# A third transform stage in three products, and stages placed otherwise over the steps of a fused FFT filter and gated FFN

## The chip, the core and the metric

The kernel runs on one core of a Trainium2 chip. The metric is device time in microseconds (us) of one execution; the median of three runs is 1530.87 us (1530.43 to 1530.92). On the core, TensorE multiplies matrices (PE in the profile; PEld is its weight load), VectorE (DVE), ScalarE (ACT) and GpSimd (POOL) work on whole tiles, and SyncE (SP) issues the DMA transfers of the steady part. Each engine takes its own instructions strictly in order.

## The reference

The input `x` has 8 batches of 3136 rows and 256 columns. Each batch goes through a Fourier filter along the rows, then through a gated feed-forward network with a convolution of width 3:

```
X = np.fft.rfft(x, axis=1)
y = np.fft.irfft(X * (filt_r + 1j * filt_i), n=3136, axis=1)
h = np.maximum(y @ w_in, 0)                      # 256 -> 1024
conv[s] = sum(conv_w[k] * h[s + k - 1] for k in 0, 1, 2)
out = (h / (1 + np.exp(-conv))) @ w_out          # 1024 -> 256
```

Everything is float32 in and out.

## The kernel before, in words

**The transform.** 3136 is 112 x 28, so the Fourier transform and its inverse are done in four stages of matrix products, each in 14 pieces (`NP`, number `q`) of 112 or 120 rows by 512. Stage 1 multiplies the input by a table from HBM and stores the result in HBM (`store_first`). Stage 2 multiplies by the constant `s2_sb`, and its result in PSUM is multiplied by the filter (`filt`): three VectorE instructions (L300 to L302) and one GpSimd addition (L303) give the tile `z`. Stage 3 multiplies `z` by the constant `s3_sb` (`by_row`, L277 and, for the last piece, L280); ScalarE copies its result out of PSUM (`store_plain`, L268) and SP stores it in HBM. Stage 4 loads that back in another order, multiplies by a table (`fourth`, L311), VectorE copies the result (L733), and ScalarE and GpSimd write `y` as a rounded high part and a rest.

**Products of parts.** A float32 number may be split in a high part that is rounded to the type `fp32r` (`hi_act`, ScalarE, L156) and the rest, the difference of number and high part (`lo_pool`, GpSimd, L162, or `lo_dve`, VectorE, L159). `mm3` (L185 to L187) replaces one float32 product by three `fp32r` products: high by high, high by rest, rest by high. The FFN uses it throughout; so does stage 2 from the third batch on (`second_split`), whose parts stage 1 has stored in two tensors, `a_dram` and `r_dram`. Stages 1, 3 and 4, and stage 2 of the second batch, are plain float32 products.

**The FFN.** The rows of all batches are cut into 50 units of 510 (`UO`), each with 8 slices (`NF`) of the 1024 hidden columns. One slice of one unit is a *step*; there are 400, numbered m. In step m, TensorE does the transform pieces planned for this step, then the first product of slice m (`inner`, 6 matmuls), then the second product of slice m-6 (`project`, 12 matmuls). The other engines do, in step m, for slices of earlier steps:

- ScalarE: relu in PSUM of slice m-1 (L557), the middle tap of m-1 (`centre`, L562, it writes a tile `t` of 4 buffers), the sigmoid of m-2 (L569), the rounding of m-3 (`round_g`, L156).
- VectorE: the two outer taps of m-1 (L566) and between them the gate of m-2 (L572, the last reader of that slice's PSUM tile `ps_h`, of which there are 3).
- GpSimd: the rest of m-4 (`rest_g`, L162), the last reader of that slice's `t`.

Whatever the transform pieces of step m-1 left in PSUM is taken out by VectorE and ScalarE at the start of their step m, ahead of the FFN work there; the GpSimd addition L303 stands ahead of `rest_g` too. Every eighth step (m mod 8 = 6) a unit is done: VectorE copies two tiles of results (`evacuate`, L611) ahead of all else in that step, and SP has their output transfers (L616, L629) ahead of this step's loads.

**The plan.** The transform of batch t (t from 1 to 7; batch 0 is transformed ahead of the steps) runs during the 48 steps from w = 48(t-1) on, in which the FFN works on batch t-1. The lists `at1`, `at2`, `at4` and the counter `used` set the step of each piece: stage 2 at 9 steps for 5 pieces from w+2 on (t = 1: 3 for 2, from 7), stage 3 three steps after its stage 2, stage 4 in steps w+33 to w+44. The 14 pieces of stage 1 of the *next* batch go where the fewest other pieces are: in every window of t from 2 on that is w+0, 1, 4, 6, 8, 10, 13, 22, 27, 29 to 32 and 45. Loads are asked for ahead by `want_in` (at most 3 tiles `tin` for stages 1 and 4), `want_table` (3 pieces ahead, 4 buffers) and `want_filter` (1 ahead, 2 buffers). Where a batch ends within a unit, `join_tail` and `join_head` put the rows of both batches into a tile `yx`.

Of the kernel before, what the change touches and what calls it, by code (L numbers as in the profile page):

```python
# [9 lines left out]
F32 = mybir.dt.float32  # L10
F32R = mybir.dt.float32r
I32 = mybir.dt.int32
# [8 lines left out]
D = 256  # L21
FF = 1024
KT = D // 128
NF = FF // 128
UO = 510
# [107 lines left out]
def tile_fft_filter_gated_ffn(  # L133
# [21 lines left out]
    def hi_act(dst, src):  # L155
        nc.scalar.activation(dst, src, AF.Copy)  # L156
# [4 lines left out]
    def lo_pool(dst, src, hi):  # L161
        nc.gpsimd.tensor_tensor(out=dst, in0=src, in1=hi.bitcast(F32), op=ALU.subtract)  # L162
# [21 lines left out]
    def mm3(ps, wh, wl, rh, rl, start=True, stop=True, **kw):  # L184
        nc.tensor.matmul(ps, lhsT=wh, rhs=rh, start=start, stop=False, **kw)  # L185
        nc.tensor.matmul(ps, lhsT=wh, rhs=rl, start=False, stop=False, **kw)  # L186
        nc.tensor.matmul(ps, lhsT=wl, rhs=rh, start=False, stop=stop, **kw)  # L187
# [12 lines left out]
    wc = ctx.enter_context(tc.tile_pool(name="wc", bufs=1))  # L200
    s2_sb = wc.tile([112, 120], F32, name="s2_sb")
    s2s_sb = wc.tile([112, 120], F32, name="s2s_sb")
    second_parts = [[wc.tile([112, 120], F32R, name=f"{n}{h}") for h in range(2)] for n in ("s2", "s2s")]
    s3_sb = wc.tile([120, 112], F32, name="s3_sb")
    s3s_sb = wc.tile([120, 112], F32, name="s3s_sb")
    cw = wc.tile([128, 3, NF], F32, name="cw")
# [1 line left out]
    nc.scalar.activation(cw[:, 0, 0:1], cw[:, 0, 0:1], AF.Sigmoid)  # L208
    wi = [wc.tile([128, KT, FF], F32R, name=f"wi{h}") for h in range(2)]
    wo = [wc.tile([128, NF, D], F32R, name=f"wo{h}") for h in range(2)]  # L210
    turned = [wc.tile([120, 2, D], F32, name=f"v{k}") for k in range(2)]
    for v in turned:
        nc.gpsimd.memset(v[32:64], 0.0)

    tp = ctx.enter_context(tc.tile_pool(name="tp", bufs=2))
# [11 lines left out]
    NP = 14  # L227
# [47 lines left out]
    def by_row(o, q, r, m, ms):  # L275
        if q < NP - 1:
            nc.tensor.matmul(o, lhsT=m, rhs=r.rearrange("p j d -> p (j d)"), start=True, stop=True)  # L277
        else:
            for j, t in ((0, m), (1, ms)):
                nc.tensor.matmul(o[:, j * D:j * D + D], lhsT=t, rhs=r[:, j], start=True, stop=True)  # L280
# [9 lines left out]
            for j, parts in enumerate(second_parts):  # L290
                mm3(ps[0:120, j * D:j * D + D], *parts, r[:, 0, j], r[:, 1, j])

    def third(ps, q, z):
        by_row(ps[0:112], q, z, s3_sb, s3s_sb)

    def filt(ps, q, f, last=False):

# [18 lines left out]

    AHEAD = 6
    raws = {}
    conv_raw = tp.tile([128, 1, 6 * NF], I32, name="conv_raw", bufs=1)

    def load_weights(k, pool):
        if pool is tp:
# [39 lines left out]
    with (  # L362
# [16 lines left out]
        def bank():  # L379
            return sps.tile([128, 512], F32, name="ps")  # L380
# [22 lines left out]
        with tc.tile_pool(name="sq", bufs=2) as sq:  # L403
# [8 lines left out]
            def tab(kind, q):  # L412
                return tabs[kind, q // 2][:, 2 * (q % 2):2 * (q % 2) + 2]
# [22 lines left out]
            for q in range(NP):  # L436
# [6 lines left out]
                ps = turned_stage(rows["x", q // 2][:, 2 * (q % 2):2 * (q % 2) + 2], [tab("1", q)[:, j] for j in range(2)])  # L443
# [11 lines left out]
            for i in range(NP + 4):  # L455
# [34 lines left out]
        for q in range(NP + 1):  # L490
# [3 lines left out]
            if q:  # L494
                ps = bank()
# [10 lines left out]
    wp = ctx.enter_context(tc.tile_pool(name="wp", bufs=2, reuse_waits="tile"))  # L506
# [6 lines left out]
    NU = -(-LEN // UO)  # L513
    ts, hs, gs, pos, joined = {}, {}, {}, {}, {}
# [9 lines left out]
    def place(u):  # L524

        b, tok = divmod(UO * u, ROW)
        return b, tok, min(UO, LEN - UO * u)

    def joins(u):
        _, tok, n = place(u)  # L530
        return tok + n > S

    def join_tail(u):
        b, tok, n = place(u)
        joined[u] = [wp.tile([128, KT, UO + 2], F32R, name=f"yx{h}", bufs=1) for h in range(2)]
        for t, y in zip(joined[u], ys[b]):
            nc.gpsimd.tensor_copy(t[:, :, 0:ROW + 1 - tok], y[:, :, tok:ROW + 1])

# [93 lines left out]
    NW = 6 * NF  # L632
    plan, tails, heads = {}, {}, {}

    def put(m, kind, b, q):
        plan.setdefault(m, []).append((kind, b, q))

    for t in range(1, B):
        w = NW * (t - 1)
        used = [0] * NW  # L640
        if t == 1:
            at1 = [q // 2 for q in range(NP - AHEAD)]
            at2, at4 = [7 + 3 * q // 2 for q in range(NP)], [34 + 11 * q // NP for q in range(NP)]
            for q, s in enumerate(at1):
                put(s, "1", 1, AHEAD + q)
                used[s] += 1
        else:
            at2, at4 = [2 + 9 * q // 5 for q in range(NP)], [33 + 12 * q // NP for q in range(NP)]
        for q in range(NP):
            for s, kind, cost in ((at2[q], "2", 3), (at2[q] + 3, "3", 1), (at4[q], "4", 1)):  # L650
                put(w + s, kind, t, q)
                used[s] += cost
        if t + 1 < B:
            spots = []
            for q in range(NP):
                s = min(range(4 if t == 1 else 0, NW - 2), key=lambda s: (used[s], s))
                used[s] += 2
                spots.append(s)
            for q, s in enumerate(sorted(spots)):
                put(w + s, "1", t + 1, q)  # L660
        tails[w + 29] = heads[w + 46] = next(u for u in range(NU) if joins(u) and place(u)[0] == t - 1)
        assert NF * tails[w + 29] >= w + NW
    order = [(m, op) for m in sorted(plan) for op in plan[m]]
    inputs = [op for _, op in order if op[0] in "124"]
    tables = [op for _, op in order if op[0] in "14"]
# [1 line left out]
    got_in, got_table, got_filter, got_z, banks, vs = {}, {}, {}, {}, {}, {}  # L667
# [18 lines left out]
    def want_table(n):  # L686
        for op in tables[n:n + 1]:
            src = {"1": s1, "4": m2}[op[0]]
            got_table[op] = t = tp.tile([112, 2, 112], F32, name="tab", bufs=4)
            nc.sync.dma_start(out=t, in_=src[0:112, pair(op[2])])  # L690

    def want_filter(n):
# [4 lines left out]
    done, wanted = {"in": 0, "table": 0, "filter": 0}, {"in": 0}  # L697
    def transform(op):
        kind, b, q = op
        banks[op] = ps = ps_t.tile([128, 512], F32, name="ps_t")  # L700
        if kind in "124":
            done["in"] += 1
            r = got_in.pop(op)
        if kind in "14":
            want_table(done["table"] + 3)
            done["table"] += 1
            w = got_table.pop(op)
        if kind == "1":
            by_column(ps, w, r)
        if kind == "2":  # L710
            want_filter(done["filter"] + 1)
            done["filter"] += 1
            (second_split if b > 1 else second)(ps, q, r)
        if kind == "3":
            third(ps, q, got_z.pop((b, q)))
        if kind == "4":
            fourth(ps, r, w)

# [16 lines left out]
    def to_y(op):  # L735
        kind, b, q = op
        if kind == "4":
            v = vs.pop(op)
            yh, yl = y_slices(b, pair(q))
            hi_act(yh, as_y(v))  # L740
            return lambda: lo_pool(yl, as_y(v), yh)
        return lambda: None

    with tc.manual_schedule(engines=COMPUTE | {mybir.EngineType.SP}):
        want_in()
        for n in range(3):
            want_table(n)
        for m in range(NF * NU + PLAG + 1):
            p1, p2, p3, p4, p6, p7 = (at(m - k) for k in (1, 2, 3, 4, PLAG, PLAG + 1))
            new, old = plan.get(m, []), plan.get(m - 1, [])  # L750
            if p7:
                evacuate(*p7)
            if m == NF:
                for (h, l), t in zip(second_parts, (s2_sb, s2s_sb)):
                    nc.gpsimd.tensor_copy(h, t)
                    lo_pool(l, t, h)
            for op in old:
                from_bank(op)
            want_in()
            if m in tails:  # L760
                join_tail(tails[m])
            if m in heads:
                join_head(heads[m])
            for op in new:
                transform(op)
            if a := at(m):
                inner(*a)
            if p1:
                relu(*p1)
                centre(*p1)  # L770
            if p2:
                sigmoid(*p2)
            if p1:
                tap(*p1, 0)
            if p3:
                round_g(*p3)
            later = [to_y(op) for op in old]
            if p2:
                gate(*p2)
            if p4:  # L780
                rest_g(*p4)
            for step in later:
                step()
            if p1:
                tap(*p1, 2)
            if p6:
                project(*p6)
            if m > 0:
                steps(early, 3)
            if m == 4:  # L790
                want_filter(0)
# [43 lines left out]
```

## Time and profile before

| | |
|---|---|
| median of 3 runs | 1530.87 us |
| the profiled execution | 1535.36 us, its span 1533.6 us |
| granted TensorE clock over the span | 0.998 |
| busy, share of the span | PE 98%, PEld 85%, DVE 80%, ACT 75%, POOL 54% |
| DMA | 268.52 MB, mean 175 GB/s |
| chain that ended last | PE 89%, DVE 4%, DMA 3%, ACT 2%, POOL 1% |

The shares are means over parts with different limits, so the text below reads stretches of a few steps. In a timeline row stand the start in us from the span's beginning, the duration, the engine, the line of the program, the operation, and the tiles: written, then read. `x2` means two instructions merged in a row. Idle time ahead of it, and what ended that, stand in square brackets. A plain float32 product of 512 columns shows as two records, a `fp32r` product as one; the ends of matmuls are modelled, so the cost of a product is read from the starts of the ones that follow. SPq rows are DMA issues.

### The profile page before, as it was taken

The page shows a single profiled execution, that of the slowest core. Times are in us where ns is not written, and L with a number is a line of the kernel's source. Part 1 is how long each engine was busy: PE and PEld are TensorE (multiplying, and loading weights), DVE is VectorE, ACT ScalarE, POOL GpSimd, SP SyncE. Part 2 cuts the span into 40 slices and gives each one's busy share as a digit, 9 for nine tenths or more (in the row PEclk, how much of TensorE's full clock was granted, in tenths as well). Part 3 has the DMA queues.
Part 4 walks back from the last instruction along what each step waited for, and adds up shares of the span by engine and source line. Part 5 has one row for each costly group of instructions (what it writes and reads, how often), then busy time and mean ns, then how long its engine had stood idle before and what let it go on. Part 6 is the DMA issues. An engine that isn't in the chain of part 4 may idle for free.

```text
span 1533.6 us, 26885 instructions
## 1 busy us (share of the span) xinstructions
PE 1506.5 (98%) x9292; PEld 1305.4 (85%) x9292; DVE 1227.3 (80%) x1886; ACT 1143.6 (75%) x1977; POOL 828.8 (54%) x720
## 2 busy tenths in 40 slices
PE   7989999999999999999999999999999999999999
PEld 6877788888998888988898888988899888989998
DVE  6978876888778887788878987788877888777776
ACT  3676678776887677876788667976688667888886
POOL 4635447545574555645565454745557455754443
PEclk9999999999999999999999999999999999999999
DMA  9867764686549756597546885388554663300001
GB/s 313 300 174 242 238 189 128 189 260 199 167 120 281 234 164 182 155 264 231 175 138 205 241 239 169 109 256 256 172 173 118 206 186 94 107 28 15 28 29 31
DMA packets 188743, 268.52 MB, mean 175 GB/s; under 512 B 19024, under 2 KB 130304, under 8 KB 188608
## 3 DMA queue, kind: packets, MB, share of 16 engines
q1 hardware_dynamic: 187168, 265.43, 57.4%
q8 instruction: 74, 1.21, 0.3%
q10 hardware_dynamic: 1440, 1.38, 0.3%
q14 instruction: 61, 0.50, 0.1%
HBM read 176.82 MB, written 89.92 MB: 174 GB/s over the span
## 4 chain that ended last, share of the span: by engine, by line
PE 89%; DVE 4%; DMA 3%; ACT 2%; issue 1%; POOL 1%; SPq 0%; ACTq 0%; DVEq 0%; POOLq 0%
PE ps_h L185 12%; PE ps_h L187 11%; PE ps_h L186 11%; PE po L598 11%; PE po L600 11%; PE po L599 11%; PE ps_t L277 6%; PE ps_t L311 5%; PE ps_t L273 4%; PE ps_t L185 1%; PE ps_t L186 1%; PE ps_t L187 1%; DVE t L566 1%; DMA r_dram<-sh 1%; PE ps L388 1%
## 5 line engine op out<-in xcount | busy, mean ns | idle before, releaser
L566 DVE SCALAR_TENSOR_TENSOR t<-ps_h,cw,t 128x510 f32<-128x510 f32 (+1 forms) x800 | 588.6, 736 | 247.7 <-ACT t L562 244.2
L162 POOL TENSOR_TENSOR g<-t,g 128x510 fp32r<-128x510 f32 (+1 forms) x400 | 506.0, 1275 | 207.2 <-ACT g L156 194.2
L598 PE MATMUL po<-wo,g 128*128 128x256 f32 (+1 forms) x1576 | 440.1, 279 | 0.1
L600 PE MATMUL po<-wo,g 128*128 128x256 f32 (+1 forms) x1576 | 439.5, 279 | 0.0
L599 PE MATMUL po<-wo,g 128*128 128x256 f32 (+1 forms) x1576 | 439.1, 279 | 0.0
L562 ACT ACTIVATE t<-ps_h,cw 128x510 f32<-128x510 f32 (+1 forms) x400 | 272.4, 681 | 148.8 <-POOL g L162 119.4
L557 ACT ACTIVATE ps_h<-ps_h 128x512 f32<-128x512 f32 (+1 forms) x400 | 235.1, 588 | 177.2 <-PE ps_h L187 174.8
L303 POOL TENSOR_TENSOR z<-z,v 120x512 f32<-120x512 f32 x111 | 144.3, 1300 | 354.4 <-DVE v L302 300.8
L185 PE MATMUL ps_h<-y,wi 128*128 128x512 f32 (+1 forms) x688 | 311.3, 453 | 2.6 <-DVE t L572 2.4
L598 PEld LDWEIGHTS po<-wo,g 128*128 128x128 f32 (+1 forms) x1576 | 297.2, 189 | 17.2 <-ACT g L156 0.3
L599 PEld LDWEIGHTS po<-wo,g 128*128 128x128 f32 (+1 forms) x1576 | 296.6, 188 | 17.2
L600 PEld LDWEIGHTS po<-wo,g 128*128 128x128 f32 (+1 forms) x1576 | 297.1, 189 | 0.5 <-POOL g L162 0.4
L186 PE MATMUL ps_h<-y,wi 128*128 128x512 f32 (+1 forms) x688 | 270.0, 392 | 0.2 <-DVE y L159 0.2
L187 PE MATMUL ps_h<-y,wi 128*128 128x512 f32 (+1 forms) x688 | 270.0, 392 | 0.0
L572 DVE TENSOR_TENSOR t<-ps_h,t 128x510 f32<-128x510 f32 (+1 forms) x400 | 268.6, 672 | 1.1 <-ACT t L569 0.8
L569 ACT ACTIVATE t<-t 128x510 f32<-128x510 f32 (+1 forms) x400 | 245.4, 613 | 3.0 <-DVE t L566 2.9
L156 ACT ACTIVATE g<-t 128x510 fp32r<-128x510 f32 (+1 forms) x400 | 245.1, 613 | 0.5 <-DVE t L572 0.2
L162 POOL TENSOR_TENSOR y<-z,y 128x448 fp32r<-128x448 f32 x98 | 138.5, 1422 | 100.4 <-ACT y L156 95.9
L185 PEld LDWEIGHTS ps_h<-y,wi 128*128 128x128 f32 x688 | 130.1, 189 | 39.9 <-DVE t L572 9.2
L186 PEld LDWEIGHTS ps_h<-y,wi 128*128 128x128 f32 x688 | 130.7, 190 | 30.2 <-issue 11.4
L187 PEld LDWEIGHTS ps_h<-y,wi 128*128 128x128 f32 x688 | 129.9, 189 | 29.9
L311 PE MATMUL ps_t<-tab,tin 112*128 112x112 f32 x784 | 102.2, 274 | 4.1 <-DVE t L566 2.3
(127 smaller groups left out, 1709.1 us busy)
## 6 DMA issues: line engine op xcount, KB each, us to landing
filt<-in_filt SPq DMA_DIRECT2D x98, 512.0 KB
tia<-a_dram SPq DMA_DIRECT2D x98, 224.0 KB
b_dram<-st SPq DMA_DIRECT2D x98, 224.0 KB
tin<-b_dram SPq DMA_DIRECT2D x98, 224.0 KB
a_dram<-sh SPq DMA_DIRECT2D x88, 224.0 KB
tin<-in_x SPq DMA_DIRECT2D x84, 224.0 KB
r_dram<-sh SPq DMA_DIRECT2D x84, 224.0 KB
tia<-r_dram SPq DMA_DIRECT2D x84, 224.0 KB
```

The source lines that it names most:

```text
L156: nc.scalar.activation(dst, src, AF.Copy)
L162: nc.gpsimd.tensor_tensor(out=dst, in0=src, in1=hi.bitcast(F32), op=ALU.subtract)
L185: nc.tensor.matmul(ps, lhsT=wh, rhs=rh, start=start, stop=False, **kw)
L186: nc.tensor.matmul(ps, lhsT=wh, rhs=rl, start=False, stop=False, **kw)
L187: nc.tensor.matmul(ps, lhsT=wl, rhs=rh, start=False, stop=stop, **kw)
L562: nc.scalar.activation(t, hs[u, f][:, 1:n + 1], AF.Copy, scale=cw[:, 1, f:f + 1])
L566: nc.vector.scalar_tensor_tensor(out=t, in0=h[:, k:place(u)[2] + k], scalar=cw[:, k, f:f + 1], in1=t, op0=ALU.mult, op1=ALU.add)
L569: nc.scalar.activation(ts[u, f], ts[u, f], AF.Sigmoid)
L572: nc.vector.tensor_mul(ts[u, f], hs.pop((u, f))[:, 1:place(u)[2] + 1], ts[u, f])
L598: nc.tensor.matmul(o, lhsT=gh[:, c:c + n], rhs=wo[0][:, f], start=first, stop=False, skip_group_check=True)
L599: nc.tensor.matmul(o, lhsT=gh[:, c:c + n], rhs=wo[1][:, f], start=False, stop=False, skip_group_check=True)
L600: nc.tensor.matmul(o, lhsT=gl[:, c:c + n], rhs=wo[0][:, f], start=False, stop=last, skip_group_check=True)
```

## The change

1. **Stage 3 in three products**, in all of the batches 1 to 7 (`third_split`). The constants `s3_sb` and `s3s_sb` get a high part and a rest (`third_parts`); these and those of stage 2 are made by eight small GpSimd instructions in step 4 (four of them, for stage 2, were made in step 8). The tile `z` is split two steps after its stage 2 (`split_z`): ScalarE writes the high part, GpSimd the rest, both of 120x512, after the other work of that step. The plain copy of `z` is then free.
2. **Places.** Stage 2 is at 8 steps for 5 pieces, from w+6 on (t = 1: from 7), stage 3 four steps after it, stage 4 in steps w+34 to w+44 (w+34, w+37 and w+40 hold two pieces). Stage 1 of the next batch is in w+0 to 5, w+28 to 33, w+45 and 46 (t = 1: steps 4, 5, 9, 14, 17, 22, 25, 28 to 33 and 46). `join_tail` is at w+33 for w+29.
3. **Memory.** The new tiles `parts` (2 buffers) also serve as the former `yx`; tables have 3 buffers and are asked for 2 ahead; the raw convolution weights use a `z` buffer; the two tiles `turned` are 8 columns longer.

```diff
+    third_parts = [[wc.tile([120, 112], F32R, name=f"{n}{h}") for h in range(2)] for n in ("s3", "s3s")]
...
-    def third(ps, q, z):
-        by_row(ps[0:112], q, z, s3_sb, s3s_sb)
+    def third_split(ps, q, r):
+
+        if q < NP - 1:
+            mm3(ps[0:112], *third_parts[0], *(r[:, h].rearrange("p j d -> p (j d)") for h in range(2)))
+        else:
+            for j, parts in enumerate(third_parts):
+                mm3(ps[0:112, j * D:j * D + D], *parts, r[:, 0, j], r[:, 1, j])
...
+    free = [*range(0, 6), *range(28, 34), 45, 46]
     for t in range(1, B):
         w = NW * (t - 1)
-        used = [0] * NW
+        for q in range(NP):
+            s2 = 7 + 8 * q // 5 if t == 1 else 6 + 8 * q // 5
+            for s, kind in ((s2, "2"), (s2 + 4, "3"), (34 + 10 * q // 13, "4")):
+                put(w + s, kind, t, q)
         if t == 1:
-            at1 = [q // 2 for q in range(NP - AHEAD)]
-            at2, at4 = [7 + 3 * q // 2 for q in range(NP)], [34 + 11 * q // NP for q in range(NP)]
...
-        else:
-            at2, at4 = [2 + 9 * q // 5 for q in range(NP)], [33 + 12 * q // NP for q in range(NP)]
...
+            for q in range(AHEAD, NP):
+                put((q - AHEAD) // 2, "1", 1, q)
         if t + 1 < B:
...
+                put(w + (free[q] if t > 1 else (4, 5, 9, 14, 17, 22, 25, 28, 29, 30, 31, 32, 33, 46)[q]), "1", t + 1, q)
-        tails[w + 29] = heads[w + 46] = next(u for u in range(NU) if joins(u) and place(u)[0] == t - 1)
+        tails[w + 33] = heads[w + 46] = next(u for u in range(NU) if joins(u) and place(u)[0] == t - 1)
...
-            want_table(done["table"] + 3)
+            want_table(done["table"] + 2)
...
+    def split_z(op):
+        z = got_z[op[1:]]
+        got_z[op[1:]] = r = wp.tile([128, 2, 2, D], F32R, name="parts", bufs=2)[0:120]
+        hi_act(r[:, 0], z)
+        return lambda: lo_pool(r[:, 1], z, r[:, 0])
...
-            if m == NF:
-                for (h, l), t in zip(second_parts, (s2_sb, s2s_sb)):
+            if m == 4:
+                for (h, l), t in zip(second_parts + third_parts, (s2_sb, s2s_sb, s3_sb, s3s_sb)):
...
-            later = [to_y(op) for op in old]
+            later = [to_y(op) for op in old] + [split_z(op) for op in plan.get(m - 2, []) if op[0] == "2"]
```

Where instructions stand, at three places. VectorE in a window of t = 2, before: the copies of a finished unit (L611) stand ahead of the three filter instructions (L300 to L302) of the same step, and a rest of stage 1 (L159) stands two lines further up.

```order
L566 SCALAR_TENSOR_TENSOR t<-ps_h,cw,t 128x510
L159 TENSOR_TENSOR sh<-ps_t,sh 112x512
L566 SCALAR_TENSOR_TENSOR t<-ps_h,cw,t 128x510
L572 TENSOR_TENSOR t<-ps_h,t 128x510
L566 SCALAR_TENSOR_TENSOR t<-ps_h,cw,t 128x510
L611 COPY ot<-po_2932 128x512
L611 COPY ot<-po_2933 128x512
L300 TENSOR_TENSOR z<-ps_t,filt 120x512
L301 TENSOR_TENSOR v_99<-ps_t,filt 56x512
L302 SCALAR_TENSOR_TENSOR v_99<-ps_t,filt 56x512
L566 SCALAR_TENSOR_TENSOR t<-ps_h,cw,t 128x510
L572 TENSOR_TENSOR t<-ps_h,t 128x510
```

With the change (lines shift by some six), at the copies of the second unit in that window:

```order
L308 SCALAR_TENSOR_TENSOR v_103<-ps_t,filt 56x512
L572 SCALAR_TENSOR_TENSOR t<-ps_h,cw,t 128x510
L578 TENSOR_TENSOR t<-ps_h,t 128x510
L572 SCALAR_TENSOR_TENSOR t<-ps_h,cw,t 128x510
L617 COPY ot<-po_3315 128x512
L617 COPY ot<-po_3316 128x512
L572 SCALAR_TENSOR_TENSOR t<-ps_h,cw,t 128x510
L578 TENSOR_TENSOR t<-ps_h,t 128x510
L572 SCALAR_TENSOR_TENSOR t<-ps_h,cw,t 128x510
L306 TENSOR_TENSOR z<-ps_t,filt 120x512
L307 TENSOR_TENSOR v_104<-ps_t,filt 56x512
L308 SCALAR_TENSOR_TENSOR v_104<-ps_t,filt 56x512
```

The copies are now in a step that has no filter instructions, and no rest of stage 1 is left among the steps with stage 2.

GpSimd in the first steps of that window with stage 2, before (`g` is the rest of an FFN slice, `z` the addition L303):

```order
L303 TENSOR_TENSOR z<-z,v_99 120x512
L162 TENSOR_TENSOR g_955<-t,g_954 128x510
L303 TENSOR_TENSOR z<-z,v_100 120x512
L162 TENSOR_TENSOR g_949<-t,g_948 128x510
L162 TENSOR_TENSOR g_951<-t,g_950 128x510
L303 TENSOR_TENSOR z<-z,v_99 120x512
```

With the change:

```order
L309 TENSOR_TENSOR z<-z,v_103 120x512
L162 TENSOR_TENSOR g_959<-t,g_958 128x510
L309 TENSOR_TENSOR z<-z,v_104 120x512
L162 TENSOR_TENSOR g_953<-t,g_952 128x510
L162 TENSOR_TENSOR parts<-z,parts 120x512
L162 TENSOR_TENSOR g_955<-t,g_954 128x510
L162 TENSOR_TENSOR parts<-z,parts 120x512
L309 TENSOR_TENSOR z<-z,v_103 120x512
```

One more GpSimd instruction (`parts`) for each piece of stage 2, always behind the `g` of its step.

SP about the outputs in the midst of stage 4 of t = 2, step w+38, before (`tin<-b_dram` loads a piece of stage 4, `tab<-in_m` its table):

```order
L629 DMA out<-ot 126x256
L251 DMA tin<-b_dram_75 112x2x256
L690 DMA tab<-in_m 112x224
L251 DMA tin<-b_dram_75 112x2x256
L690 DMA tab<-in_m 112x224 x2
L251 DMA tin<-b_dram_75 112x2x256 x2
```

With the change:

```order
L635 DMA out<-ot 126x256
L252 DMA tin<-b_dram_75 112x2x256 x2
L686 DMA tab<-in_m 112x224
L252 DMA tin<-b_dram_75 112x2x256
L686 DMA tab<-in_m 112x224
L252 DMA tin<-b_dram_75 112x2x256
```

Two loads of stage 4 now follow the outputs of step w+38 at once, where one did.

More of the change, by code (lines that the diff above doesn't have):

```diff
@@ L210, in tile_fft_filter_gated_ffn @@
     wo = [wc.tile([128, NF, D], F32R, name=f"wo{h}") for h in range(2)]
-    turned = [wc.tile([120, 2, D], F32, name=f"v{k}") for k in range(2)]
+    turned = [wc.tile([120, 2 * D + 8], F32, name=f"v{k}")[:, 0:2 * D].rearrange("p (j d) -> p j d", d=D) for k in range(2)]
     for v in turned:
@@ L318, in tile_fft_filter_gated_ffn @@
     raws = {}
-    conv_raw = tp.tile([128, 1, 6 * NF], I32, name="conv_raw", bufs=1)
+    conv_raw = tp.tile([128, 1, 2 * D], F32, name="z", bufs=3).bitcast(I32)[:, :, 0:6 * NF]
     def load_weights(k, pool):
@@ L534, in join_tail @@
         b, tok, n = place(u)
-        joined[u] = [wp.tile([128, KT, UO + 2], F32R, name=f"yx{h}", bufs=1) for h in range(2)]
+        joined[u] = [wp.tile([128, 2, 2, D], F32R, name="parts", bufs=2).rearrange("p a j d -> p a (j d)") for _ in range(2)]
         for t, y in zip(joined[u], ys[b]):
@@ L636, in put @@
         plan.setdefault(m, []).append((kind, b, q))
+    free = [*range(0, 6), *range(28, 34), 45, 46]
     for t in range(1, B):
         w = NW * (t - 1)
-        used = [0] * NW
+        for q in range(NP):
+            s2 = 7 + 8 * q // 5 if t == 1 else 6 + 8 * q // 5
+            for s, kind in ((s2, "2"), (s2 + 4, "3"), (34 + 10 * q // 13, "4")):
+                put(w + s, kind, t, q)
         if t == 1:
-            at1 = [q // 2 for q in range(NP - AHEAD)]
-            at2, at4 = [7 + 3 * q // 2 for q in range(NP)], [34 + 11 * q // NP for q in range(NP)]
-            for q, s in enumerate(at1):
-                put(s, "1", 1, AHEAD + q)
-                used[s] += 1
-        else:
-            at2, at4 = [2 + 9 * q // 5 for q in range(NP)], [33 + 12 * q // NP for q in range(NP)]
[L649 to L652, printed above, removed]
+            for q in range(AHEAD, NP):
+                put((q - AHEAD) // 2, "1", 1, q)
         if t + 1 < B:
-            spots = []
             for q in range(NP):
[L656 to L660, printed above, removed]
-        tails[w + 29] = heads[w + 46] = next(u for u in range(NU) if joins(u) and place(u)[0] == t - 1)
-        assert NF * tails[w + 29] >= w + NW
+                put(w + (free[q] if t > 1 else (4, 5, 9, 14, 17, 22, 25, 28, 29, 30, 31, 32, 33, 46)[q]), "1", t + 1, q)
+        tails[w + 33] = heads[w + 46] = next(u for u in range(NU) if joins(u) and place(u)[0] == t - 1)
+        assert NF * tails[w + 33] >= w + NW
     order = [(m, op) for m in sorted(plan) for op in plan[m]]
@@ L688, in want_table @@
             src = {"1": s1, "4": m2}[op[0]]
-            got_table[op] = t = tp.tile([112, 2, 112], F32, name="tab", bufs=4)
+            got_table[op] = t = tp.tile([112, 2, 112], F32, name="tab", bufs=3)
             nc.sync.dma_start(out=t, in_=src[0:112, pair(op[2])])
@@ L714, in transform @@
         if kind == "3":
-            third(ps, q, got_z.pop((b, q)))
+            third_split(ps, q, got_z.pop((b, q)))
         if kind == "4":
@@ L742, in to_y @@
         return lambda: None
+    def split_z(op):
[3 more added lines that the diff above has]
+        return lambda: lo_pool(r[:, 1], z, r[:, 0])
     with tc.manual_schedule(engines=COMPUTE | {mybir.EngineType.SP}):
         want_in()
-        for n in range(3):
+        for n in range(2):
             want_table(n)
```

## The prediction

> **What bounds the kernel now.** I read the page's head and chain first, then TensorE's waits, then a window of steps.
>
> ```profile
> span 1533.6 us, 26885 instructions
> PE 89%; DVE 4%; DMA 3%; ACT 2%; issue 1%; POOL 1%; SPq 0%; ACTq 0%; DVEq 0%; POOLq 0%
> PE ps_h L185 <- DVE t L572: 2.4, 7, 0.7
> 459.94:642.01 182.07, 181.07 (x1109) 157.49 (x1108) 147.53 (x226) 137.57 (x236) 100.00 (x84) 1.00 0.66 198
> ```
>
> The chain is TensorE's for 89% of the span; its longest wait for the FFN in the steps is a sum of 2.4 us; and in the 48 steps of the window t = 3 (last row: length, then busy PE, PEld, DVE, ACT, POOL) it is busy 181.07 of 182.07 us. So a product saved counts in full as long as nothing else becomes the limit. VectorE with 147.5 us seems far off. But this is an average: its work lies where stage 2 is.
>
> **Prices on TensorE.** The timeline, where steps 72 to 73 begin and inside a stage 2, and the first slices of steps 340 and 392, between which no transform is left:
>
> ```profile
> 359.98 0.39 PE L187 MATMUL ps_t<-tia,s 112*120 112x512 f32 x1
> 360.21 0.40 PE L185 MATMUL ps_h<-y,wi 128*128 128x512 f32 x1
> 371.05 1.02 PE L277 MATMUL ps_t<-z,s_sb 120*112 120x512 f32 x2
> 372.15 0.40 PE L186 MATMUL ps_h<-y,wi 128*128 128x512 f32 x1
> 1367.73 0.39 PE L185 MATMUL ps_h<-y,wi 128*128 128x512 f32 x1
> 1512.37 0.21 PE L185 MATMUL ps_h<-y,wi 128*128 128x108 f32 x1
> ```
>
> One fp32r product takes 360.21 - 359.98 = 0.23 us, three 0.70. From the plain stage 3 to the second product behind it are 1.10 us, of which one product is 0.23: it costs 0.87. A step without transform is (1512.37 - 1367.73) / 52 = 2.78. So a piece saves 0.87 - 0.70 = 0.167, and 7 x 14 = 98 pieces **16.4 us**. The last piece of each batch, in halves, is priced alike; stages 1 and 2 (plain) are products of as many columns, so 0.87 too.
>
> The Trainium skill ("FP8 and Floating Point Precision", section TensorE Precision Notes) says that a true float32 product takes four passes; an estimate of three quarters of 0.87 would make the saving 0.22 a piece, 21 us in all. The rows above have 0.23 for a pass as a product of its own, and I go by them.
>
> **The added instructions.** High part and rest of 120x512 are not in the trace; the nearest are those of 128x510:
>
> ```profile
> L162 POOL TENSOR_TENSOR g<-t,g 128x510 fp32r<-128x510 f32 x392 | 502.8, 1292 | 199.2 <-ACT g L156 188.9 <-POOL g L162 3.8 <-DVE t L572 2.5
> L156 ACT ACTIVATE g<-t 128x510 fp32r<-128x510 f32 x392 | 242.8, 619 | 0.2 <-PE po L599 0.2
> ```
>
> 98 x 1.29 = 127 us more on POOL and 98 x 0.62 = 61 us on ACT. Both have room by their sums; whether they lengthen anything depends on the loop below.
>
> **The loop that the places run into.** Filter work in a step reaches round over four engines. Rows of steps 72 to 74, where stage 2 comes every other step, then of steps 51 to 53, where it comes twice running:
>
> ```profile
> 371.20 0.68 DVE L300 TENSOR_TENSOR z<-ps_t,filt 120x512 f32<-120x512 f32 x1
> 373.37 1.30 POOL L303 TENSOR_TENSOR z<-z,v 120x512 f32<-120x512 f32 x1 [3.58 <-DVE v L302]
> 374.62 2.55 POOL L162 TENSOR_TENSOR g<-t,g 128x510 fp32r<-128x510 f32 x2
> 375.95 0.69 ACT L562 ACTIVATE t<-ps_h,cw 128x510 f32<-128x510 f32 x1 [1.81 <-POOL g L162]
> 376.67 0.75 DVE L566 SCALAR_TENSOR_TENSOR t<-ps_h,cw,t 128x510 f32<-128x510 f32 x1 [1.35 <-ACT t L562]
> 378.59 0.68 DVE L300 TENSOR_TENSOR z<-ps_t,filt 120x512 f32<-120x512 f32 x1
> ...
> 287.20 0.74 DVE L566 SCALAR_TENSOR_TENSOR t<-ps_h,cw,t 128x510 f32<-128x510 f32 x1
> 287.86 0.68 DVE L300 TENSOR_TENSOR z<-ps_t,filt 120x512 f32<-120x512 f32 x1
> 291.89 0.68 DVE L300 TENSOR_TENSOR z<-ps_t,filt 120x512 f32<-120x512 f32 x1
> 298.63 0.74 DVE L566 SCALAR_TENSOR_TENSOR t<-ps_h,cw,t 128x510 f32<-128x510 f32 x1
> ```
>
> VectorE ends L302, POOL adds (L303), and only then makes the rest of an FFN slice, which frees the `t` that ACT's L562 waits for; VectorE's tap waits for that, its idle 1.35 us. Nothing in it waits for TensorE. A step with filter work and one without take 378.59 - 371.20 = 7.39 us. Two with and one without take 298.63 - 287.86 = 10.77 to the last tap, and 0.66 until VectorE goes on behind it (287.86 - 287.20): 11.43.
>
> With the change, in each window from t = 2 on, the filter work lies in steps 7, 8, 10, 11, 13, 15, 16, 18, 19, 21, 23, 24, 26, 27 (from w): in the 22 steps 7 to 28 six groups of three and two of two, 6 x 11.43 + 2 x 7.39 = **83.4 us**. TensorE has there 22 x 2.78, 13 pieces of stage 2 and 12 of stage 3 at 0.70, and one stage 1 at 0.87: **79.5 us**. It was more before, since pieces of stage 1 stood between, and stage 3 took 0.87. Now the loop is the longer by 3.9.
>
> What can TensorE take of this lag? The last batch has no stage 1 to place, and shows it already (steps 305 to 307):
>
> ```profile
> 1244.59 1.02 PE L277 MATMUL ps_t<-z,s_sb 120*112 120x512 f32 x2
> 1245.55 0.68 DVE L300 TENSOR_TENSOR z<-ps_t,filt 120x512 f32<-120x512 f32 x1
> 1248.24 0.40 PE L185 MATMUL ps_t<-tia,s 112*120 112x512 f32 x1
> 1251.98 1.02 PE L277 MATMUL ps_t<-z,s_sb 120*112 120x512 f32 x2
> 1252.92 0.68 DVE L300 TENSOR_TENSOR z<-ps_t,filt 120x512 f32<-120x512 f32 x1
> ```
>
> TensorE's two steps take 7.39, the loop's time, where its work is 2 x 2.78 + 0.70 + 0.87 = 7.13; VectorE's filter work begins 0.96 after TensorE's step. So from a lag of about 0.96 on TensorE waits (for the gate L572, the last reader of `ps_h`). And at the start? Step w+6 copies a unit out, as step 126 does:
>
> ```profile
> 573.58 1.37 DVE L611 COPY ot<-po 128x512 f32<-128x512 f32 x2 [0.65 <-PE po L600]
> 574.06 1.03 PE L273 MATMUL ps_t<-tin,tab 112*112 112x256 f32 x4
> 576.72 0.74 DVE L566 SCALAR_TENSOR_TENSOR t<-ps_h,cw,t 128x510 f32<-128x510 f32 x1
> ```
>
> VectorE is free 576.72 + 0.66 - 574.06 = 3.32 after TensorE's step began; with stage 2 that step lasts 3.48, so VectorE enters step 7 ahead by 0.16. Lag at the end 3.9 - 0.16 = 3.7, less 0.96: TensorE waits some **2.8 us** in each of the batches t = 2 to 6, 14.0 in all. Ends: nothing, if the loop is shorter than these rows, and 3.9. In the last batch the pace was the loop's before; the saving is partly void there: 1.0 (0 to 3.9). In t = 1 stage 2 is plain (0.87) and five pieces of stage 1 stay among it: 13 x 0.17 + 5 x 0.87 = 6.6 more for TensorE, 86.1. The loop has 83.4 and the copies of two units (1.37 each, rows above), which there fall on steps with filter work: about level, and I take nothing (0 to 2).
>
> The new rest (1.29) does not enter the loop: it stands behind the `g` of its step. In a group of three POOL has 2 additions, 3 `g` and 2 new rests, 7 x 1.3 = 9.1 of 11.43 us, and the stage 3 that waits for them comes three VectorE steps after the filter work. That is the cover; without it see the third rival.
>
> **Stage 4 behind the outputs.** In step w+38 SP issues the outputs of a unit, then loads. Rows of steps 134 and 135, and of steps 38 and 39 (t = 1, whose step w+37 already holds two pieces of stage 4, as all will):
>
> ```profile
> 605.47 1.04 PE L311 MATMUL ps_t<-tab,tin 112*128 112x112 f32 x8
> 607.33 0.35 SPq L251 DMA_DIRECT2D tin<-b_dram  x1
> 609.17 1.04 PE L311 MATMUL ps_t<-tab,tin 112*128 112x112 f32 x8
> 610.42 0.78 PE L311 MATMUL ps_t<-tab,tin 112*128 112x112 f32 x5 [0.21 <-DMA tin<-b_dram]
> ...
> 241.88 0.89 SPq L251 DMA_DIRECT2D tin<-b_dram  x2
> 245.10 1.11 PE L311 MATMUL ps_t<-tab,tin 112*128 112x112 f32 x8 [1.75 <-DVE t L566]
> ```
>
> The first load behind the outputs is issued 1.86 after the step's start and used 3.1 later, at 610.42. Before, it was the *second* piece of step w+39, at hand 0.36 late (610.42 - 609.17 - 0.89). With the change it is the first, wanted at 609.17: 1.25 late. In t = 1 such a wait was 1.75. Net 0.9 to 1.4; near the row of the same load I take 1.0, times six batches: **6.0 us**. Ends: 0 and 1.75 x 6 = 10.5. The pairs in w+34 and w+40 I take as before, since a pair stood at w+33 and at w+39; three a window for two, ahead of a queue without outputs, so at nothing (up to 0.36 x 7 = 2.5).
>
> **The start.** POOL makes eight small parts ahead of its first `g`, where four came later:
>
> ```profile
> 104.88 1.28 POOL L162 TENSOR_TENSOR g<-t,g 128x510 fp32r<-128x510 f32 x1
> 108.03 0.69 ACT L562 ACTIVATE t<-ps_h,cw 128x510 f32<-128x510 f32 x1
> 113.83 0.29 POOL L755 CAST s<-s_sb 112x120 fp32r<-112x120 f32 x1
> 114.95 0.44 POOL L162 TENSOR_TENSOR s2s<-s2s_sb,s2s 112x120 fp32r<-112x120 f32 x1
> ```
>
> Four take 115.39 - 113.83 = 1.56, eight 3.1: the first `g` ends at 109.3, and the L562 that then needs its `t` begins 1.2 late: 1.0 us (0 to 3.1). The table buffer less, the later `join_tail` and the shared tiles touch no chain that I could find: 0.
>
> **Sum:** -16.4 + 14.0 + 1.0 + 6.0 + 1.0 = +5.6 us against the profiled span of 1533.6 (its run took 1535.36, the median of the runs is 1530.87; the difference is taken over): **1536.5 us**.
>
> **Rivals.**
>
> 1. *TensorE stays the limit and the saving comes out* (0.27). The loop shortens or the lag is caught up in pieces; the windows lose nothing: -16.4 + 6.0 + 1.0 = 1521.5. For it: the chain with 89% and the window t = 1, with pairs of stage 2 in two steps of three and no wait. Against: there TensorE had 0.87 for each, and the last batch shows the loop.
> 2. *No change* (0.20): the windows lose as I say, but the load lands in time, for example since less traffic lies beside it: -16.4 + 14.0 + 1.0 = 1529.5.
> 3. *POOL enters the loop* (0.05): ACT's high part comes late, the new rest is still running when L302 ends, and the addition waits. It decides from 2.3 us later than I reckon (11.43 - 9.1). At 0.65 a group, 8 groups and 6 batches: 31 us more, 1567.
> 4. *The change does not do what it says* (0.03): three products with new weights each cost TensorE as much as the plain one: 16.4 more, 1553.
>
> The forecast itself has 0.45, with a range of its own of 1532 to 1541.
>
> **How the numbers follow.** A measurement can tell about 0.2% (3.1 us) from no change. Faster by more: rival 1 and a little of rival 2, 0.30. Within: the rest of rival 2 and the lower end of the forecast, 0.24. Slower: 0.46. The range from 1521 to 1546 leaves out most of rivals 3 and 4 and the outer part of rival 1; its upper end is the forecast with 3.9 a window for 2.8 and a wait of 1.75 in stage 4.
>
> **What would show it.** Right: stage 3 costs 0.70; in the windows t = 2 to 6 TensorE's waits for L572 or L566 grow by 2 to 3 us between w+20 and w+29, VectorE's L300 follow at 7.39 or 11.43; a wait of 1 to 2 us ahead of the first L311 (now L317) of w+39. Wrong: TensorE without a gap in these steps, or POOL's addition waiting for POOL.

## The result, and the profile after

The changed kernel takes 1582.14 us (median of four runs, 1576.74 to 1583.66), the kernel before 1530.89 beside it: a ratio of 1.0326 (95% interval 1.0300 to 1.0352). I had forecast slower, but by 5.6 us and not by 51. The profiled execution took 1576.74 us, so its trace holds some 41 of the 51.

The page of the changed kernel: its head, POOL's addition, and a group of instructions that is new (busy time and mean ns, then idle time ahead of it):

```profile
span 1575.0 us, 27325 instructions
PE 1506.3 (96%) x9397; PEld 1328.2 (84%) x9397; DVE 1226.5 (78%) x1886; ACT 1188.6 (75%) x2075; POOL 952.6 (60%) x822
L309 POOL TENSOR_TENSOR z<-z,v 120x512 f32<-120x512 f32 x111 | 142.9, 1288 | 215.7 <-DVE v L308 207.1
L162 POOL TENSOR_TENSOR parts<-z,parts 120x512 fp32r<-120x512 f32 x98 | 127.1, 1297 | 16.4 <-issue 16.2
```

The new rest costs what I took from its neighbour, 1.30 us, and POOL's addition L309 waits for VectorE, not for POOL. In TensorE's and VectorE's waits (sum, times, longest) stands what is wrong:

```profile
PE ps_h L185 <- DVE t L578: 31.7, 19, 3.4
PE ps_t L274 <- DMA tab<-in_s: 6.6, 5, 2.7
PE ps_t L317 <- DMA tin<-b_dram: 5.1, 4, 1.9
...
DVE z L306 <- DMA filt<-in_filt: 29.4, 17, 3.0
```

TensorE waits 31.7 us for the gate (2.4 before). That alone could be the loop that I forecast. The last row could not: VectorE waits 29.4 us, 17 times, for a load of the filter. Before, the trace has for this wait:

```profile
DVE z L300 <- DMA filt<-in_filt: 1.5, 3, 0.9
```

One case, steps w+6 to w+9 of the window t = 3: SP's queue, then VectorE, then TensorE in the timeline of the changed kernel.

```profile
489.21 0.40 SPq L622 DMA_DIRECT2D out<-ot  x1
489.89 0.84 SPq L635 DMA_DIRECT2D out<-ot  x2
490.83 0.34 SPq L262 DMA_DIRECT2D a_dram<-sh  x1
491.26 0.41 SPq L265 DMA_DIRECT2D r_dram<-sh  x1
491.72 0.49 SPq L691 DMA_DIRECT2D filt<-in_filt  x1
...
495.67 0.74 DVE L572 SCALAR_TENSOR_TENSOR t<-ps_h,cw,t 128x510 f32<-128x510 f32 x1
498.18 0.69 DVE L306 TENSOR_TENSOR z<-ps_t,filt 120x512 f32<-120x512 f32 x1 [1.78 <-DMA filt<-in_filt]
...
501.71 0.50 PE L185 MATMUL ps_h<-y,wi 128*128 128x512 f32 x1 [2.16 <-DVE t L578]
```

Step w+6 puts a unit out (of the steps with stage 2, w+6, w+14 and w+22 do), and the change, from t = 2 on, starts pairs of stage 2 exactly there: w+6 and 7, w+14 and 15, w+22 and 23. The program asks for each filter one piece ahead, inside the step of the piece before; so the filter for the *second* piece of these pairs is asked for in the very step that puts the unit out, behind the unit's outputs, which wait for VectorE's copies (in w+6 also behind two stores of stage 1, L262 and L265). It is issued at 491.72 and used at 498.18, 6.5 us later. VectorE, in order, stands 1.78 us with its taps and gates behind it, and TensorE 2.16.

Behind such a stop comes a second loss. Two stretches of the same kernel, cut at the borders at which the clock can change (busy time of PE, PEld, DVE, ACT, POOL, then granted clock, DMA share, GB/s):

```profile
499.55:502.97 3.42, 1.26 (x6) 1.05 (x6) 2.71 (x5) 0.28 (x2) 2.61 (x3) 1.00 0.76 192
502.97:506.38 3.41, 3.41 (x16) 3.19 (x15) 2.75 (x5) 3.32 (x7) 3.41 (x3) 0.50 0.60 181
```

TensorE idles 2.16 of 3.42 us, and in the next 3.41 us it has half the clock: a half-rate period. The trace has nine of them in the steps, before it had two: 7 more, each worth 3.41 / 2 = 1.7 us at most, some 12 us. The mean clock says the same: 0.990 for 0.998, 0.008 x 1575 = 12.6 us.

By batches (48 steps each, from the starts of TensorE's steps) the window t = 3 went from 182.1 to 190.1 us, and the windows t = 2 to 6 lost 42.8 us together; t = 1 and the last batch are within 2 us of before.

### The profile page after: what moved, and what is told of

Its sections match the earlier page's. It is cut to its first block, busy times and chain, and to the rows that moved or that the text cites. A ratio compares the mean times of both kernels' runs of the same rounds, so it can differ in the third digit from the quotient of the medians.

```text
span 1575.0 us, 27325 instructions
## 1 busy us (share of the span) xinstructions
PE 1506.3 (96%) x9397; PEld 1328.2 (84%) x9397; DVE 1226.5 (78%) x1886; ACT 1188.6 (75%) x2075; POOL 952.6 (60%) x822
## 5 line engine op out<-in xcount | busy, mean ns | idle before, releaser
L185 PE MATMUL ps_h<-y,wi 128*128 128x512 f32 (+1 forms) x688 | 297.8, 433 | 31.9 <-DVE t L578 31.7
L309 POOL TENSOR_TENSOR z<-z,v 120x512 f32<-120x512 f32 x111 | 142.9, 1288 | 215.7 <-DVE v L308 207.1
L162 POOL TENSOR_TENSOR parts<-z,parts 120x512 fp32r<-120x512 f32 x98 | 127.1, 1297 | 16.4 <-issue 16.2
```

## The experiments

The loss has four candidates: the late filter load, the loop over four engines that I had forecast, the late loads of stage 4, and the table that stage 1 waits for ahead of step w+5 (the expectations count this wait, and that at the start, to the step that ends with it: w+4, and step 5 for step 6). None of these kernels leaves work out. Medians, and ratios to the kernel before with their 95% intervals:

| kernel | us | ratio |
|---|---|---|
| places alone, plain stage 3 | 1584.41 | 1.0350 (1.0328 to 1.0373) |
| changed kernel | 1582.14 | 1.0326 (1.0300 to 1.0352) |
| one step later | 1564.38 | 1.0213 (1.0189 to 1.0237) |
| filter first, plain stage 3 | 1554.28 | 1.0158 (1.0139 to 1.0177) |
| filter first | 1548.70 | 1.0120 (1.0102 to 1.0137) |
| all loads first | 1535.45 | 1.0034 (1.0019 to 1.0049) |
| all loads first, stage 1 spread, plain stage 3 | 1526.36 | 0.9966 (0.9948 to 0.9984) |
| kernel before, all loads first | 1524.39 | 0.9953 (0.9937 to 0.9970) |
| all loads first, addition later | 1518.78 | 0.9916 (0.9901 to 0.9931) |
| all loads first, stage 1 spread | 1511.98 | 0.9876 (0.9860 to 0.9892) |
| the three together | 1508.71 | 0.9844 (0.9827 to 0.9860) |
| the three, constants' parts later | 1506.96 | 0.9836 (0.9814 to 0.9858) |

**1. The filter load ahead of the outputs.**

```diff
+            if p7 and p7[1] == NF - 1 and any(op[0] == "2" for op in new):
+                want_filter(done["filter"] + 1)
             if p7:
                 evacuate(*p7)
```

(`want_filter` skips what has been asked for already.)

> The filter load for the second piece of a pair is asked for ahead of the outputs of a unit, in the steps w+6, w+14 and w+22; nothing else differs from the changed kernel (median 1582.1 us). Theory A (the late filter loads cost most of what I missed: TensorE's 31.7 us of waits for the gate, and the half-rate clock periods behind those of 2 us and more): the 17 waits of VectorE for the filter are gone, of the waits for the gate about the 14 us stay that the loop over four engines was reckoned to cost, and some 6 clock periods of 1.7 us go: 31.7 - 14 + 10 = 28 us less, about 1554. Rival B (the loop over VectorE, ACT and POOL costs it, and the filter waits only lie inside its slack): at most 5 us less, 1577 or more, and the waits for the gate stay near 30 us.

Measured: 1548.70, 33.4 us less. Its timeline in the same step, and its waits:

```profile
482.83 0.35 SPq L696 DMA_DIRECT2D filt<-in_filt  x1
487.07 0.41 SPq L622 DMA_DIRECT2D out<-ot  x1
```

```profile
PE ps_h L185 <- DVE t L578: 8.1, 21, 2.3
```

SP issues the load 4.0 us before the step begins (486.83) and 4.2 before the unit's first output; the wait for it is gone, TensorE's waits for the gate are 8.1 us for 31.7, and no half-rate period is left behind the start (step 6). One line of order in SP's queue was worth two thirds of the loss. Theory A holds, with more than its 28 us. (The two profiled executions, 1576.74 and 1551.27 us, are 25.5 apart.)

**2. The same cause from the other side: one number in the places.**

```diff
-            s2 = 7 + 8 * q // 5 if t == 1 else 6 + 8 * q // 5
+            s2 = 7 + 8 * q // 5
```

> The changed kernel with one number else: stage 2 (and stage 3 behind it) one step later from t = 2 on, at w+7, 8, 10, 11, 13, 15, 16, ... as in t = 1. The order of the loads is the changed kernel's. Now no piece of stage 2 falls in a step in which a unit is put out (w+6, 14, 22), so no filter load stands behind outputs. Theory (that coincidence is what costs it): VectorE's waits for the filter go as with the filter load ahead, and some 30 us with them; VectorE's copies of two units now fall on steps with filter work, 2 to 10 us back: 1549 to 1560. Rival (the filter load is late because of the density of stage 2 or of what else SP has to do, not because of the outputs): about 1582.

Measured: 1564.38, 17.8 us less, with the order of loads as in the changed kernel. The filter waits are gone here too, and so are the half-rate periods:

```profile
DVE z L306 <- DMA filt<-in_filt: 1.8, 2, 1.1
...
PE ps_h L185 <- DVE t L578: 15.5, 31, 1.6
```

It is the coincidence of pairs and outputs, not the density of stage 2. The price of moving was above my range: many short waits for the gate (the copies now fall on steps with filter work), and 1.2 to 1.7 us ahead of the second piece of stage 4 in w+34, in five of seven windows; stage 4 now comes three steps behind the last stage 3, not four.

**3. Places alone, and the three products alone.** Stage 3 plain again (`by_row` on the unsplit `z`, no `split_z`), once in the changed kernel, once with the filter load ahead:

```diff
-            third_split(ps, q, got_z.pop((b, q)))
+            by_row(ps[0:112], q, got_z.pop((b, q)), s3_sb, s3s_sb)
...
-            later = [to_y(op) for op in old] + [split_z(op) for op in plan.get(m - 2, []) if op[0] == "2"]
+            later = [to_y(op) for op in old]
```

> The changed kernel with its places and its order of loads, but stage 3 as one plain product of the unsplit z. Theory: the places cost it all, and the three products give back as little as in the pair of runs with the filter load ahead (5.6 us), so 1582 + 5.6 = 1588. Rival: the added parts of ACT and POOL make part of the 50 us (their work in the loop): then this is faster than 1582, down to 1547 if the places cost no more than the saving.

> The run with the filter load ahead of the outputs, but stage 3 as one plain product of the unsplit z, as before the change: no high part by ACT, no rest by POOL, the places of the change. If TensorE's saving of 0.167 us a piece came out everywhere, this is 16.4 us slower than the same kernel with three products (about 1570 if that is at 1554). If the loop is the limit between w+7 and w+28, the 12 pieces that lie there in each of five windows save nothing, and the difference is 16.4 - 5 x 12 x 0.167 = 6.4 us. If ACT's and POOL's new instructions disturb the loop, it is no slower at all, or faster.

Measured: 1584.41 and 1554.28. The places cost all of it; the three products gave back about 2 us there, where 5.6 was expected (the two ratios overlap), and 5.6 with the filter load in time, where 6.4 was expected if the loop swallows the pieces between w+7 and w+28. That the loop swallows most of them is better read from the profiles of the second pair: steps w+7 to w+28 of the windows t = 2 to 6 differ by 0.4 us each, where 12 pieces of 0.167 make 2.0. That the total comes so near to 6.4 is in part luck: the two profiles differ by 6.5 us, and their steps w to w+5 alone by 6.6, since in the windows t = 3, 4 and 5 of the kernel with the plain stage 3 a half-rate period follows the wait for the table.

**4. All loads of the step ahead of the outputs.**

```diff
             if p7 and p7[1] == NF - 1:
+                if any(op[0] == "2" for op in new):
+                    want_filter(done["filter"] + 1)
+                if any(op[0] in "14" for op in new):
+                    want_table(done["table"] + 2)
+                want_in()
```

> In the steps in which a unit is put out, the filter, the next table and the inputs that the step asks for are all asked for ahead of the outputs. Theory: beside the filter waits the waits of stage 4 at w+38 and w+39 (0.9 to 1.9 us in each of 7 windows, about 9 us with their clock periods) go, 9 us less than with the filter load alone, about 1545; the wait for a table at w+4 (0.8 to 1.5 us) stays, since it stands behind loads, not behind outputs. Rival: the loads only move the lateness to the outputs or to one another, and the time is that with the filter load alone.

Measured: 1535.45 (1532.30 to 1541.31 in ten runs), 13.2 us less than with the filter alone, where 9 was expected. Step w+39 of t = 3, with the filter load alone ahead (first row) and with all of them (second):

```profile
615.27 1.12 PE L317 MATMUL ps_t<-tab,tin 112*128 112x112 f32 x8 [2.06 <-DMA tin<-b_dram]
```

```profile
611.76 1.04 PE L317 MATMUL ps_t<-tab,tin 112*128 112x112 f32 x8
```

Steps w+34 to w+39 fall from 183.2 to 170.7 us over the seven windows; the waits ahead of w+39, 0.81 to 2.18 us, were 10.0 of that. The wait ahead of w+5 stays, as expected.

**5. The same edit in the kernel before.**

> The kernel before the change (1530.6 us), with the one edit of the run with all loads ahead of the outputs. Theory: with the old places hardly any load that a step needs stood behind outputs (VectorE's waits for the filter and TensorE's waits for inputs sum to under 3 us there, plus one wait of 1.75 in t = 1), so 0 to 4 us less, 1527 to 1531. Rival: the order of the loads is worth the same 13 us here as between the two runs of the changed kernel, 1517, and then the split has no part in the best time.

Measured: 1524.39, 7.5 us less: more than the 0 to 4 expected, well short of 13. Most of it, 4.8 us, lies in t = 1, where the wait of 1.75 at w+39 and the half-rate period behind it go. So the old places hid the order of the queue, not quite wholly.

**6. The loop: fill TensorE's waiting.** On top of experiment 4, some pieces of stage 1 between those of stage 2:

```diff
-    free = [*range(0, 6), *range(28, 34), 45, 46]
+    free = [0, 1, 2, 3, 8, 11, 16, 19, 24, 28, 30, 32, 45, 46]
```

> As the run with all loads ahead of the outputs, and from t = 2 on five pieces of stage 1 (of w+4, 5, 29, 31 and 33) stand in steps w+8, 11, 16, 19 and 24, between the pieces of stage 2. Theory (the loop over four engines sets the pace between w+7 and w+28, at 83.4 us, and TensorE has 79.5 of work there): the 5 x 0.87 = 4.35 us of stage 1 take the place of TensorE's waiting there and leave the other steps that much shorter: some 3 us less in each of five windows, and the wait for the table at w+4 (about 1 us in each) goes too: 15 to 20 us less than without, about 1528. Rival (the loop is not the limit once the loads come in time): only the table wait goes, some 5 us.

Measured: 1511.98, 23.5 us less, where 15 to 20 was expected. The window t = 3 in three stretches, steps w to w+5, w+6 to w+28, w+29 to w+33, first with all loads ahead, then also spread:

```profile
462.70:485.93 23.23, 22.09 (x134) 19.47 (x133) 15.46 (x24) 16.81 (x31) 7.75 (x6) 1.00 0.80 242
485.93:571.63 85.70, 84.76 (x501) 72.27 (x500) 76.31 (x117) 62.50 (x116) 61.12 (x49) 1.00 0.70 205
571.63:591.28 19.65, 19.65 (x121) 17.44 (x120) 16.00 (x25) 16.87 (x32) 11.04 (x14) 1.00 0.85 253
```

```profile
451.70:471.80 20.10, 20.10 (x126) 17.97 (x125) 14.87 (x23) 15.74 (x29) 7.76 (x6) 1.00 0.77 235
471.80:559.16 87.36, 87.36 (x522) 76.54 (x520) 80.70 (x123) 68.21 (x125) 63.34 (x51) 1.00 0.81 239
559.16:576.21 17.05, 17.05 (x109) 15.29 (x108) 12.48 (x19) 13.70 (x25) 8.86 (x12) 1.00 0.66 195
```

Five pieces, 4.35 us of work, lengthen the middle by only 1.66: 2.7 us of them fit in TensorE's waiting. (The first kernel's row counts only 0.94 us there as idle; the ends of matmuls are modelled, and the rest of the waiting must stand there as busy.) The third stretch loses 2.60 (3 pieces of 0.87), the first 3.13, of which 1.74 is two pieces and 1.4 the wait for the table. TensorE's row now leaves no gap in any of the three.

**7. The loop: take POOL's addition out of it.**

```diff
             if p4:
                 rest_g(*p4)
+            while adds:
+                adds.pop(0)()
```

(Also on top of experiment 4; `filt` puts its addition in the list `adds` and doesn't issue it.)

> As the run with all loads ahead of the outputs (1535.5 us), but POOL makes the filter's addition (1.3 us) behind the rest of g of the same step, not ahead of it; so a step with filter work no longer holds up the tile t that ACT waits for. Theory (the loop VectorE, POOL's addition, POOL's rest of g, ACT, VectorE sets the pace of the steps w+6 to w+28, 85.6 us in the profile for 83.7 us of TensorE's work): the loop falls below TensorE's work, and these steps take 83.7: 1.9 us less in each of five windows and some 1 us in the other two, 11 to 12 less, about 1524. Rival 1: something else than the addition sets the loop's pace, and nothing changes. Rival 2: z and its rest come 1.3 us later, and stage 3 waits for them: slower than 1535.

Measured: 1518.78, 16.7 us less. The stretch w+6 to w+28 of t = 3:

```profile
477.79:561.33 83.54, 83.26 (x501) 72.89 (x500) 78.30 (x119) 66.76 (x120) 63.88 (x51) 1.00 0.72 212
```

83.54 us for 85.70, and 166.0 for 169.0 in the last batch. So the loop is what I said it was, and in the five windows it cost 1.9 to 2.3 us each. Some 3 us of the 16.7, in steps w+34 to 39 and elsewhere, I have not traced.

**8. Both, and the plain stage 3 with TensorE as the limit.**

> The three edits together: all loads ahead of the outputs, stage 1 spread, and the filter's addition behind the rest of g. Theory: with stage 1 spread TensorE is already the limit in the windows (its batches take 178 us for 48 x 2.78 + 14 x 0.87 + 28 x 0.70 + 14 x 0.89 = 177.8 us of work), so the shorter loop has nothing left to give from t = 2 to 6; only the last batch, which has no stage 1, gains its 3 us: 1509. Rival: the two gains (23.5 and 16.7 us) add, 1495.

> As the run with all loads ahead of the outputs and stage 1 spread (1512.0 us), but with stage 3 as one plain product of the unsplit z. Theory: TensorE is the limit there in all windows, and every one of the 98 pieces counts: 98 x 0.167 = 16.4 us more, 1528. Rival: the loop over the four engines still sets the pace of 12 pieces in each of five windows, and only 6 us of the saving show, 1518.

Measured: 1508.71 and 1526.36. The two gains of 23.5 and 16.7 do not add: with stage 1 spread TensorE is the limit, and only the last batch (166.0 for 169.0 us) gains by the shorter loop. And there the three products are worth 14.4 us, near the 16.4 of the plain sum. In the profiles the batches t = 1 to 6 differ by 14.5 us, 0.173 a piece; the last by 0.6 only, where the loop holds.

**9. The start.** The eight small parts, two at a time in steps 4 to 7 behind the rest of `g` and not all in step 4, on top of the three edits:

```diff
+            if 4 <= m < 8:
+                (h, l), t = list(zip(third_parts + second_parts, (s3_sb, s3s_sb, s2_sb, s2s_sb)))[m - 4]
+                nc.gpsimd.tensor_copy(h, t)
+                lo_pool(l, t, h)
```

> The three edits together (1508.7 us), and POOL makes the eight small parts of the constants two at a time, behind the rest of g of steps 4 to 7, not all eight ahead of the first rest of g in step 4. Theory (these eight delay the gate at step 5, where the changed kernel's TensorE waits 1.80 us and the kernel before 0.25, and the clock falls to half for a period behind it): 1.5 to 4 us less, 1505 to 1507. Rival (the start is late from its loads, and this wait lies in the shadow of those of steps 1 and 2): the same, 1509.

Measured: 1506.96 (1504.67 to 1507.93) for 1508.71 (1507.03 to 1511.94): 1.75 us less, at the edge of what the runs tell apart; and ahead of step 6 TensorE still waits 1.13 us, so the parts are not all of that wait. This is the fastest kernel of the study, 1.6% below the kernel before; the order of the loads alone is worth 0.5% at the old places (experiment 5). The later addition was not tried there. In its window t = 3 TensorE has no gap:

```profile
450.29:628.14 177.85, 177.85 (x1125) 159.14 (x1123) 147.23 (x226) 145.44 (x250) 117.82 (x97) 1.00 0.69 202
```

The three products at the *old* places were not tried: the `parts` tiles hold the joined unit into step w+7 of the next window, so stage 2 from w+2 on finds no buffer.

## Why the prediction was right or wrong

**Stage 3 at 0.70 a piece: right.** In the changed kernel:

```profile
510.36 0.39 PE L185 MATMUL ps_t<-parts,s 120*112 120x512 f32 x1
510.59 0.39 PE L186 MATMUL ps_t<-parts,s 120*112 120x512 f32 x1
510.82 0.39 PE L187 MATMUL ps_t<-parts,s 120*112 120x512 f32 x1
511.05 0.39 PE L185 MATMUL ps_h<-y,wi 128*128 128x512 f32 x1
```

511.05 - 510.36 = 0.69. With TensorE as the limit the whole kernel gets 14.4 of the 16.4 us (experiment 8). The Trainium skill's rule of four passes ("FP8 and Floating Point Precision", section TensorE Precision Notes), from which I estimated that a piece would save 0.22, is further off than the row's 0.167: the batches showed 0.173.

**The loop, 2.8 us in each of five windows: right in kind, 1.9 to 2.3 measured** with the addition out of it (experiment 7), and 2.7 us of room for other work in t = 3 (experiment 6). I gave as a sign that the waits for the gate grow by 2 to 3 us between w+20 and w+29. The changed kernel has 0.99 to 2.31 there, but from the other cause: with the loads in time the trace shows some 0.3 us a window. The loop was the only cause that I gave the windows, and it was the smaller one.

**What failed: nothing was put down for the loads of stage 2.** The step that places the filter work ("The loop that the places run into") follows L302, L303, rest of `g`, ACT and tap, and takes it that VectorE's first filter instruction waits for nothing but VectorE. The filter's load is not even among the things that are put at nothing ("touch no chain that I could find: 0" names the table buffer, `join_tail` and the shared tiles). The second operand of that instruction comes by DMA, from a queue in which outputs stand. I did ask that question of stage 4, one paragraph further on, and not of stage 2, whose load is bigger (512 KB for 224) and which the change moves on top of three output steps. The evidence was in the profile of before: SP's rows give the order, its unit outputs come in steps w+6, 14 and 22, and the old pairs from t = 2 on (w+2 and 3, 11 and 12, 20 and 21) start in none of them; the one piece in an output step, w+14, is followed two steps later. In t = 1 one old pair, w+22 and 23, did start in such a step, and there the trace of before has the whole chain in small: the filter of its second piece is issued behind the outputs, 5.6 us before its use, and VectorE waits 0.89 us, its longest wait for a filter in that trace.

```profile
176.54 0.84 SPq L629 DMA_DIRECT2D out<-ot  x2
178.36 0.48 SPq L695 DMA_DIRECT2D filt<-in_filt  x1
183.94 0.69 DVE L300 TENSOR_TENSOR z<-ps_t,filt 120x512 f32<-120x512 f32 x1 [0.89 <-DMA filt<-in_filt]
```

That term is -33.4 us when undone. Part of it came by the clock, for which the sum has no term at all: seven half-rate periods, 12 us at most. The range did not hold it, because no bound was set for a cost that I put at nothing.

**Stage 4 behind the outputs, 6.0: right, in kind and near in size.** In the changed kernel TensorE waits ahead of step w+39 of t = 2 to 7 for 0.92 to 1.88 us, 1.20 on average, where I reckoned 1.25; and t = 1, which I left out because it had 1.75 already, has 1.01. The 13.2 us of experiment 4 are more than this term. They are measured with the filter load in time, when these waits are 1.43 on average over all seven windows, and they are what the order of the loads costs in all, not what the change added to it: the same edit takes 7.5 us off the kernel before.

**The table buffer less, at nothing: wrong, as far as the rows show.** TensorE waits ahead of step w+5 in five windows, 0.8 to 1.5 us:

```profile
485.29 1.09 PE L274 MATMUL ps_t<-tin,tab 112*112 112x256 f32 x4 [1.54 <-issue]
```

The profile does not name the releaser in this row; in the window t = 5 it names `tab`. Its table is issued in step w+3 behind six loads of stage 2; asked for three ahead, it would have been due a step earlier, ahead of them. That is argued: no run had three ahead at the new places, and the six pieces of stage 1 in a row, also new, are a rival. Fewer pieces early, in experiment 6, took 1.4 us a window off. With the filter load ahead these waits sum to 6.7 us, half of what that kernel still loses beyond the forecast (18.1 us to the kernel before, for 5.6).

**The start, 1.0: within its range.** TensorE waits 1.80 ahead of step 6, where it waited 0.25 before. Experiment 9 got 1.75 back by the medians, but left a wait of 1.13.

**The last batch, 1.0: too small, within its range.** Of 14 x 0.167 = 2.3 us the three products gave it 0.6 (experiment 8), so 1.7 was void.

**The rivals.** The first (1521.5) needs a TensorE that stays the limit: that came about only with the loads ahead and stage 1 spread or the addition later. The second fell, since the load of stage 4 was late. The third fell: POOL's addition waits for VectorE for 207.1 of its 215.7 us. So did the fourth, with the row above. None of the four had a late filter.

## What to carry to other kernels

When steps of a plan are moved, list for each engine what data its first instruction needs, and where in which queue the transfer stands in the *new* place; do it for every load of the step, not for the ones that were already late. In this kernel a load that was asked for one step ahead of its use came in time only where no output, which waits for an engine, stood ahead of it in its queue; so put loads ahead of outputs. And a saving on the limiting engine comes out only where enough of its work is left between the pieces of the next loop: here spreading five pieces of stage 1 was worth more than the saving itself.

## What the runs showed of the hardware

The clock changes only at borders of a fixed grid of 3.413 us: all half-rate periods in the 13 traces start on one grid each. What decides, as far as these traces show, is the idle share of one such stretch, not the length of a stop. Laying TensorE's idle time over the grid from the first step of the FFN to step 399, I find that all 25 stretches with 57% or more idle were followed by half the clock, none with 48% or less was, and between them 8 of 14 were; what decided among those I do not know. The stop of 2.31 us that ends at 565.92 in the changed kernel is longer than the 2.16 shown above, and cost no clock, because a border divides it (idle 0.80 and 1.51 of 3.41):

```profile
561.00:564.41 3.41, 2.61 (x18) 2.02 (x16) 1.99 (x3) 3.21 (x6) 0.01 (x1) 1.00 1.07 263
564.41:567.82 3.41, 1.90 (x10) 1.64 (x11) 2.08 (x5) 0.72 (x2) 3.26 (x3) 1.00 0.99 333
567.82:571.23 3.41, 3.41 (x24) 3.07 (x24) 3.38 (x6) 3.32 (x7) 3.01 (x3) 1.00 0.06 23
```

So stops of 1.2 to 1.6 us cost their own length (44 of them, none halved), and from about 1.7 on each may cost another 1.7. The Trainium skill ("TensorE: Matmul & The Clock Gate", Part 1: The HAM clock gate) has the same free-running window of 3413 ns, which these traces bear out, but says that the clock falls after at least one idle window; here 57% of one always sufficed, and sometimes 49%.
